# A new written-out order for 2455 events, and 214 zero products in place of 240, in a delta-rule attention with a feed-forward layer

## The chip, the core and the metric

The kernel runs on one core of a Trainium2 chip. The core has five engines with a queue of their own: PE (TensorE, matrix products), DVE (VectorE), ACT (ScalarE), POOL (GpSimd) and SP (SyncE, which here only issues DMAs). Each engine works its queue in order; an instruction that waits holds up all behind it. The metric is the device time of one execution in microseconds (us), the median of several; lower is better.

## The reference

```
k_n = k / (norm(k) + 1e-6)                      # 4 batches, 8 heads, 768 steps, 48 wide
for t in range(768):                            # state is 48 x 48 for each batch and head
    y[t]  = q[t] @ state
    v_old = k_n[t] @ state
    state = state + beta[t] * outer(k_n[t], v[t] - v_old)
x = y as 3072 tokens x 384
h = x @ w_in                                    # 384 x 2048
out = (h * erf(softplus(h))) @ w_out            # 2048 x 384
```

## The kernel before

**Attention.** The 768 steps are cut into 12 chunks of 64. For a chunk c the kernel loads k (`load_step`), its transpose (`load_kf`) and q (`load_q`), forms products of keys with keys and with queries on PE (`gram_mm`, names pg and pq), scales them on DVE (`gram_a`, `gram_p`), sends the result through DRAM to another layout (`to_dram`, `to_blocks`, tile gb) and solves a triangular system of 31 rows, two chunks at a time (`solve_row`): chunks 0 and 1 on DVE, all others on POOL. `back_t`, `merge_*` put the inverse together; `chain_u`, `chain_s`, `chain_y` carry the state from chunk to chunk, one event for each chunk and batch.

**Weights.** w_in and w_out come as 12 pieces of 512 KB each (`w_load`). ACT rescales each (`w_mask`, `w_sign`), DVE joins the bits (`w_bits`), and `w_mx` (ACT, one piece on DVE) takes the largest value. From the maximum of all twelve, `w_max`, `w_all` (a product on PE) and `w_scale` make one scale, which `w_idsc`, `w_hi`, `w_lo1` and the rest need to split the weights into two 16-bit parts. The first solve, `solve_row` of group 0, stands on DVE behind `w_scale` of w_in.

**Feed-forward.** Four chain events make one group of 256 tokens, 12 groups. `x_max` to `x_lo` scale and split the group. `ffn1` (9 products) gives 128 of the 2048 columns; two such make a unit of 512 values in one of two PSUM buffers (ph). For each unit ACT does Softplus (`e_sp`), then Erf (`e_erf`); the two need different function tables, and a table load stands wherever the function changes (line 165). DVE multiplies (`e_mul`, which frees ph), `e_split` and `e_rest` make the 16-bit parts H, and `ffn2` (6 products) adds to the output.

**Zero products.** `warm`, `fill` (line 180) and `fill2` (line 186) multiply zeros by zeros, 128x128 by 128x512. No result uses them. 15 stand at the start; the other 240 are events that stand in the order wherever PE is thought to wait.

**The order.** Every piece of work is an event. The list of events is built with due times, but these are not used for the order: the tuple ORDER names the events one by one, and each puts its instructions at the end of its engine's queue. ENG names the 17 events that do not run on their usual engine.

```
for i in range(WU):
    on(us(6 + 0.17 * i), fill)
for i in range(WV):
    on(us(6 + 0.17 * (WU + i)), fill2)
...
ev = [ev[i] for i in ORDER] if ORDER else sorted(ev, key=lambda e: e[:2])
for _, i, fn in ev:
    cur[0] = i
    fn()
```

A DMA on SP also waits until the DMA eight places ahead of it in the queue has landed, and until its buffer is free: for w_in there are six buffers of one kind (H) and five of another (L).

Of the kernel before, what the change touches and what calls it, by code (L numbers as in the profile page):

```python
# [46 lines left out]
DZ = 64
WG = -6
WU = 177
WV = 63  # L50
MT = 58
M1 = 0
WL = (0.9, 0.95, 1.0, 1.05, 1.1, 1.15, 24, 24.1, 31.0, 32.5, 34.0, 35.5)
WK = (6.0, 6.7, 7.4, 8.1, 8.8, 9.5, 28, 29, 36.0, 37.5, 39.0, 40.5)
WF = (6.6, 7.3, 8.0, 8.7, 9.4, 10.1, 28.6, 29.6, 36.6, 38.1, 39.6, 41.1)
WI = (17.0, 18.0, 19.0, 20.0, 21.0, 22.0, 31, 32, 50.5, 52.1, 53.7, 55.3)
WOT = (36, 38, 40, 42, 76, 78, 62, 86, 88, 90, 72, 74)
WD = 0.4
# [28 lines left out]
def delta_ffn_kernel(ctx, tc, kT, qT, ktok, vtok, btok, w_in, w_out, cst, out):  # L87
# [20 lines left out]
    def on(t, fn, *a, **kw):  # L108
        ev.append((t, len(ev), lambda: fn(*a, **kw)))
# [24 lines left out]
    def us(x):  # L134
        return (x - T0) / SW
# [671 lines left out]
    on(-98, warm, WARM)  # L807
# [4 lines that stand above are left out]
    on(us(0), clear_q)  # L812
# [229 lines left out]
```

## Time and profile before

| what | value |
|---|---|
| median of 3 runs | 613.57 us (609.68 to 617.38) |
| the profiled execution | 615.59 us, of which the span of instructions is 613.8 us |
| PE busy in the span | 595.4 us (97%), 49.5 us of it `warm` and `fill`, 15.8 us `fill2` |
| ACT busy | 522.9 us (85%), 216.8 us of it 169 table loads of line 165 |
| DVE busy | 403.8 us (66%) |
| POOL busy | 307.8 us (50%) |

The first product of the feed-forward that goes on without a wait starts at 97.35 us. Lines are those of the kernel file: 697 is `ffn1`, 749 to 751 `ffn2`, 719 `e_sp`, 724 `e_erf`, 728 `e_mul`, 685 `x_lo`, 355 and 357 `solve_row`, 301 `gram_a`, 287 and 291 `gram_mm`, 558 `w_load`. A busy PE may be busy with zeros, so its share says little; what counts is when useful products can run.

### The profile page before, as it was taken

What the parts mean: (1) busy time and instruction counts of PE and PEld (TensorE: products, weight loads), DVE (VectorE), ACT (ScalarE), POOL (GpSimd) and SP (SyncE); (2) the same over time, 40 slices, a digit from 0 to 9 for tenths busy, and PEclk for the clock granted to TensorE, in tenths of its full rate; (3) what the DMA queues carried; (4) which work ended last, traced back from release to release, by engine and by line L of the source; (5) the groups of instructions that cost most, each with busy time, mean ns of one, the idle gap of its engine ahead of it and who ended that gap; (6) DMA issues with size and microseconds to landing.
All of it is one profiled execution on the core that took longest, in us unless ns stands there. A gap on an engine that the chain in (4) does not pass through costs nothing.

```text
span 613.8 us, 25249 instructions
## 1 busy us (share of the span) xinstructions
PE 595.4 (97%) x11019; PEld 426.9 (70%) x11019; DVE 403.8 (66%) x926; ACT 522.9 (85%) x751; POOL 307.8 (50%) x484
## 2 busy tenths in 40 slices
PE   9899989999999899999999999999999999999996
PEld 3654456667777677777777777777777777777773
DVE  0769986668787788887776977666565655436221
ACT  8859897999996789878968999897989797989873
POOL 3000313798589733998527884489953122213221
PEclk9799898999999899999999999999999999999999
DMA  9999625850755367624485226713045200100111
GB/s 313 281 235 350 152 52 124 226 141 28 185 105 142 93 163 153 156 63 117 92 212 140 67 66 148 148 50 91 1 115 121 53 17 21 27 2 14 27 27 26
DMA packets 86382, 69.72 MB, mean 114 GB/s; under 512 B 64064, under 2 KB 73408, under 8 KB 86272
## 3 DMA queue, kind: packets, MB, share of 16 engines
q1 hardware_dynamic: 86272, 68.12, 43.1%
q8 instruction: 86, 1.41, 1.0%
q14 instruction: 24, 0.20, 0.1%
HBM read 48.17 MB, written 18.87 MB: 109 GB/s over the span
## 4 chain that ended last, share of the span: by engine, by line
PE 72%; POOL 7%; DVE 5%; DMA 5%; ACT 5%; issue 4%; SPq 1%; POOLq 0%; DVEq 0%; ACTq 0%
PE ph L697 25%; PE pr L749 9%; PE pr L751 9%; PE pr L750 9%; PE warm L180 3%; POOL xb L357 3%; POOL tmptmpg L355 2%; PE pc L485 2%; DMA qp<-qT 2%; PE pc L511 2%; PE pm L448 2%; DMA k<-ktok 2%; PE pc L515 2%; PE pc L499 2%; PE pg L291 1%
## 5 line engine op out<-in xcount | busy, mean ns | idle before, releaser
L165 ACT ACT_TABLE_LOAD x169 | 216.8, 1283 | 3.0
L697 PE MATMUL ph<-xh,w_in 128*128 128x256 f16 x1152 | 206.8, 274 | 0.1
L697 PEld LDWEIGHTS <-w_in 128*128 128x128 f16 x1728 | 166.5, 98 | 30.5 <-issue 2.2
L697 PE MATMUL ph<-xl,w_in 128*128 128x256 f16 x576 | 157.8, 274 | 1.2 <-DVE xl L685 1.2
L118 POOL TENSOR_TENSOR H<-L,H 128x512 f16<-128x512 f32 x58 | 69.3, 1203 | 134.6 <-DVE H L125 89.8
L749 PE MATMUL pr<-w_out,H 128*128 128x384 f16 x384 | 126.1, 328 | 0.0
L750 PE MATMUL pr<-w_out,H 128*128 128x384 f16 x384 | 125.7, 327 | 0.0
L751 PE MATMUL pr<-w_out,H 128*128 128x384 f16 x384 | 125.7, 327 | 0.0
L728 DVE SCALAR_TENSOR_TENSOR L<-ph,L 128x512 f32<-128x512 f32 x96 | 65.8, 687 | 88.9 <-ACT L L724 74.7
L118 POOL TENSOR_TENSOR z<-v,nm 64x192 f32<-64x192 f32 x94 | 51.8, 551 | 99.9 <-DMA v<-vtok 86.0
L357 POOL TENSOR_TENSOR xb<-xb,tmptmpg 128x31 f32<-128x31 f32 (+15 forms) x154 | 90.7, 589 | 12.1
L355 POOL TENSOR_TENSOR tmptmpg<-gb,xb 128x31 f32<-128x31 f32 (+15 forms) x154 | 83.6, 543 | 24.4 <-DMA gb<-d 11.2
L719 ACT ACTIVATE L<-ph,xct 128x512 f32<-128x512 f32 x96 | 65.4, 687 | 29.3 <-PE ph L697 25.9
L724 ACT ACTIVATE L<-L 128x512 f32<-128x512 f32 x96 | 59.9, 629 | 0.9
L751 PEld LDWEIGHTS <-H 128*128 128x128 f16 x384 | 37.6, 98 | 25.1 <-issue 0.2
L749 PEld LDWEIGHTS <-H 128*128 128x128 f16 x384 | 37.5, 98 | 22.8 <-issue 0.2
L750 PEld LDWEIGHTS <-H 128*128 128x128 f16 x384 | 37.6, 98 | 20.2 <-issue 0.2
L180 PE MATMUL warm<-zero 128*128 128x512 f16 x192 | 49.5, 412 | 1.2 <-DVE zero L171 1.2
L491 DVE TENSOR_TENSOR z<-pc,ga 64x192 f32<-64x192 f32 x88 | 31.2, 355 | 18.1 <-PE pc L485 16.4
L123 ACT CAST H<-L 128x512 f16<-128x512 f32 x56 | 33.5, 610 | 8.0 <-DVE L L728 7.9
L504 DVE TENSOR_TENSOR z<-pc,z 48x192 f32<-48x192 f32 x80 | 28.3, 353 | 17.3 <-PE pc L499 14.0
L180 PEld LDWEIGHTS <-zero 128*128 128x128 f16 x192 | 18.9, 104 | 25.6 <-issue 7.2
(159 smaller groups left out, 857.1 us busy)
## 6 DMA issues: line engine op xcount, KB each, us to landing
raw_in<-w_in SPq DMA_DIRECT2D x12, 512.0 KB, 7.1
raw_out<-w_out SPq DMA_DIRECT2D x12, 512.0 KB, 6.5
d<-A SPq DMA_DIRECT2D x22, 256.0 KB, 3.4
d<-pp SPq DMA_DIRECT2D x10, 512.0 KB, 3.7
qp<-d SPq DMA_DIRECT2D x20, 256.0 KB, 4.9
k<-ktok SPq DMA_DIRECT2D x12, 384.0 KB, 4.9
kpg<-kT SPq DMA_DIRECT2D x24, 192.0 KB, 4.5
qp<-qT SPq DMA_DIRECT2D x24, 192.0 KB, 3.6
```

The source lines that it names most:

```text
L118: {"V": ve, "G": ge}[pick(d)].tensor_tensor(*a, **kw)
L165: se.add_instruction(mybir.InstLoadActFuncSet(name=nc.get_next_instruction_name(), act_func_set_id=i, ins=[], outs=[]))
L180: te.matmul(wp[0], zero[:, :P], zero, start=True, stop=True)
L355: eng.tensor_tensor(tv, G[:, s, s + 1:].unsqueeze(1).broadcast_to([P, ncol, nr]), Xv[:, :, s:s + 1].broadcast_to([P, ncol, nr]), op=ALU.mult)
L357: eng.tensor_tensor(Xv[:, :, s + 1:], Xv[:, :, s + 1:], tv, op=ALU.add)
L697: te.matmul(ph, w[:, i, kt * P:kt * P + P], G[x][:, :, ksl], start=(m == 0), stop=(m == 8))
L719: se.activation(unit(g, u), G["ph", u], AF.Softplus, bias=0.0, scale=G["ct"])
L724: se.activation(Lu, Lu, AF.Erf, bias=0.0, scale=1.0)
L728: ve.scalar_tensor_tensor(Lu, fg[g]["ph", u], HSC, Lu, op0=ALU.mult, op1=ALU.mult)
L749: te.matmul(G["po"][a], gh[:, o, asl], wout_h[:, i, :], start=(i == 0), stop=False)
L750: te.matmul(G["po"][a], gh[:, o, asl], wout_l[:, i, :], start=False, stop=False)
L751: te.matmul(G["po"][a], gl[:, o, asl], wout_h[:, i, :], start=False, stop=(i == NFF - 1))
```

## The change

ORDER is a new permutation; the numbers of WU and WV fall from 177 and 63 to 167 and 47, so 26 zero products are gone. All other events are the same, and as 26 events fewer stand ahead of most, their numbers in ORDER and ENG fall by up to 26. The 17 events of ENG are the same and on the same engines.

```diff
-ORDER = (1321,1,1276,1266,2,3,4,5,
...
+ORDER = (222,1265,1280,1260,1,1250,224,1267,1251,1252,2,3,4,5,
...
-ENG = {350: "G", 464: "V", 734: "A", 742: "A",
...
+ENG = {324: "G", 438: "V", 708: "A", 716: "A",
...
-WU = 177
-WV = 63
+WU = 167
+WV = 47
```

On PE, 83 zero products stand ahead of the first useful product where 73 stood. Behind the first `ffn1` pair there stood 5 of line 180 and 63 of line 186; now there stand 1 and 47. The first place to look at is PE near the start, the products of `gram_mm` for chunks 0 and 1 (pg and pr2 are key by key; pr0 key by query, which needs qp, the loaded q). Before, where 16 rows alternate between the two halves of qp:

```order
L287 MATMUL pg1_0_284<-kpg1_200 64x64 x16
L287 MATMUL pg0_0_304<-kpg0_301 64x64 x16
L287 MATMUL pr0_81<-qp0_0_86,kpg0_301 64x64
L287 MATMUL pr0_81<-qp0_1_87,kpg0_301 64x64
...
L287 MATMUL pg0_1_345<-kpg0_301 64x64 x16
L287 MATMUL pr2_83<-kpg1_200 64x64 x16
```

Now, with 12 zero products between the fourth row and the fifth:

```order
L287 MATMUL pr2_83<-kpg1_117 64x64 x16
L287 MATMUL pg1_0_310<-kpg1_117 64x64 x16
L287 MATMUL pg0_0_336<-kpg0_329 64x64 x16
L287 MATMUL pg0_1_355<-kpg0_329 64x64 x16
...
L287 MATMUL pr0_81<-qp0_0_86,kpg0_329 64x64
L287 MATMUL pr0_81<-qp0_1_87,kpg0_329 64x64
...
L548 MATMUL spin_494<-ident_84,m1_in_106 128x128
```

The two products with q that stood among the key products now stand behind them all. Between the key products and the next ones with q there stood 22 zero products; now there stand 12, and then 16 ahead of the product of `w_all` (spin), where 10 stood.

On SP, the start of the queue (kpg is the transposed k, k the keys, raw_in a piece of w_in, qp the loaded q, d the way out through DRAM). Before:

```order
L558 DMA raw_in1_270<-w_in 128x1024
L275 DMA kpg0_301<-kT 48x1024 x2
L218 DMA qp0_0_86<-qT 48x1024
L218 DMA qp0_1_87<-qT 48x1024
L558 DMA raw_in3_384<-w_in 128x1024
L199 DMA mask_85<-cst 128x64
L200 DMA ident_84<-cst 128x128
L558 DMA raw_in10_391<-w_in 128x1024
L558 DMA raw_in5_393<-w_in 128x1024
L218 DMA qp1_0_88<-qT 48x1024
L218 DMA qp1_1_89<-qT 48x1024
```

Now:

```order
L275 DMA kpg0_329<-kT 48x1024 x2
L558 DMA raw_in1_333<-w_in 128x1024
L558 DMA raw_in7_375<-w_in 128x1024
L558 DMA raw_in10_383<-w_in 128x1024
L558 DMA raw_in9_387<-w_in 128x1024
L218 DMA qp0_0_86<-qT 48x1024
L218 DMA qp0_1_87<-qT 48x1024
L218 DMA qp1_0_88<-qT 48x1024
L218 DMA qp1_1_89<-qT 48x1024
```

All twelve pieces of w_in now stand ahead of q, and mask and ident moved to the seventh and eighth place of the queue.

On ACT, units 5 and 6 of the first group (L719 is Softplus, L724 Erf). Before:

```order
L165 ACT_TABLE_LOAD
L719 ACTIVATE L0_2_2072<-ph0_5_2025,xct0_1349 128x512
...
L724 ACTIVATE L0_2_2072<-L0_2_2072 128x512
...
L719 ACTIVATE L0_3_2190<-ph0_6_2168,xct0_1349 128x512
...
L724 ACTIVATE L0_3_2190<-L0_3_2190 128x512
```

Now:

```order
L165 ACT_TABLE_LOAD
L719 ACTIVATE L0_2_2045<-ph0_5_1985,xct0_1407 128x512
...
L719 ACTIVATE L0_3_2151<-ph0_6_2084,xct0_1407 128x512
L165 ACT_TABLE_LOAD
L724 ACTIVATE L0_2_2045<-L0_2_2045 128x512
...
L724 ACTIVATE L0_3_2151<-L0_3_2151 128x512
```

The two Softplus now stand ahead of the two Erf, with two table loads where there were four. The same is done for units 2 and 3 and units 6 and 7 of group 1, and units 0 and 3 of group 10: 8 loads fewer, 162 in all with the first one, where there were 170.

## Rows read from the trace of the kernel before

**Rows 1.** Busy time by stretch: us, then PE, PEld, DVE, ACT, POOL, clock, DMA share, GB/s.
```profile
20.00:24.00 4.00, 2.45 (x49) 2.02 (x47) 3.32 (x7) 3.73 (x8) 0.00 (x0) 0.81 1.02 247
24.00:28.00 4.00, 4.00 (x80) 4.00 (x79) 2.88 (x8) 3.21 (x9) 0.00 (x0) 0.50 0.95 322
28.00:32.00 4.00, 4.00 (x28) 1.96 (x25) 2.99 (x6) 3.51 (x8) 0.00 (x0) 0.50 0.71 173
...
38.40:66.40 28.00, 27.94 (x247) 14.47 (x245) 24.72 (x77) 22.02 (x43) 1.11 (x2) 1.00 0.98 313
66.40:97.30 30.90, 26.05 (x860) 16.78 (x859) 28.05 (x78) 25.82 (x64) 8.46 (x14) 0.94 0.32 78
97.30:165.00 67.70, 66.71 (x1164) 47.06 (x1164) 46.49 (x98) 63.47 (x84) 49.04 (x82) 0.97 0.54 138
165.00:272.00 107.00, 103.51 (x2566) 77.54 (x2563) 89.14 (x204) 89.83 (x132) 74.11 (x125) 0.98 0.55 133
272.00:613.70 341.70, 335.50 (x5866) 250.86 (x5866) 197.38 (x432) 289.71 (x371) 169.27 (x251) 1.00 0.30 71
```

**Rows 2.** The same stretch, zero products of line 186 alone: PE, PEld, clock, DMA.
```profile
97.30:165.00 67.70, 15.81 (x63) 5.58 (x63) 0.97 0.54 138
```

**Rows 3.** The same stretch, zero products of line 180 alone.
```profile
97.30:165.00 67.70, 1.25 (x5) 0.41 (x5) 0.97 0.54 138
```

**Rows 4.** The same stretch, table loads of line 165 alone, on ACT.
```profile
97.30:165.00 67.70, 30.79 (x24) 0.97 0.54 138
```

**Rows 5.** The chain of waits in order of time: start us, us, what.
```profile
14.74 8.85 DMA qp<-qT
23.73 1.83 PE pr L287 x29
...
29.08 6.67 PE warm L180 x22
...
37.76 2.27 PE warm L180 x10
...
97.35 3.59 PE ph L697 x17
...
103.94 2.07 PE ph L697 x18
...
107.60 1.08 PE pr L186 x5
```

**Rows 6.** SP in order of time: start us, us, line, out<-in.
```profile
17.98 0.33 SPq L200 DMA_DIRECT2D ident<-cst  x1
22.19 0.80 SPq L558 DMA_DIRECT2D raw_in<-w_in  x2
```

**Rows 7.** DMA issues of the page: count, KB each, us to landing.
```profile
raw_in<-w_in SPq DMA_DIRECT2D x12, 512.0 KB, 7.1
...
qp<-qT SPq DMA_DIRECT2D x24, 192.0 KB, 3.6
```

**Rows 8.** ACT in order of time; idle time before, and what ended it, in brackets.
```profile
30.00 0.67 ACT L565 ACTIVATE w_in<-raw_in 128x512 f32<-128x512 f32 x1 [0.49 <-DMA raw_in<-w_in]
...
35.96 0.66 ACT L587 ACTIVATE raw_in<-w_in 128x512 f32<-128x512 f32 x1
...
101.69 1.28 ACT L165 ACT_TABLE_LOAD   x1
102.98 0.63 ACT L724 ACTIVATE L<-L 128x512 f32<-128x512 f32 x1
```

**Rows 9.** DVE in order of time.
```profile
38.42 0.14 DVE L596 TENSOR_REDUCE m_in<-mx_in 128x1 f32<-128x1 f32 x1
...
40.29 0.29 DVE L612 TENSOR_REDUCE m_in<-spin 128x1 f32<-128x128 f32 x1 [1.08 <-PE spin L548]
...
42.18 0.18 DVE L355 TENSOR_TENSOR tmpT<-gb,xb 128x31 f32<-128x31 f32 x1
```

**Rows 10.** PE's own waits from 97.3 us on: us in total, times, longest.
```profile
PE pc L515 <- issue: 2.8, 2, 2.3
```

More of the change, by code (lines that the diff above doesn't have):

```diff
@@ L35 @@
-ENG = {350: "G", 464: "V", 734: "A", 742: "A", 759: "V", 766: "A", 796: "A", 913: "V", 1027: "V", 1134: "V", 1295: "V", 1437: "V", 1441: "G", 1445: "G", 1639: "A", 1981: "V", 2151: "V"}
+ORDER = (222,1265,1280,1260,1,1250,224,1267,1251,1252,2,3,4,5,6,7,8,9,10,11,12,13,14,15,16,17,18,19,20,21,22,23,24,25,26,27,28,29,30,31,32,33,34,35,36,37,38,39,40,41,42,43,44,45,46,47,48,49,50,51,1269,52,53,54,55,56,57,58,59,223,60,61,62,63,64,65,66,67,68,69,70,1253,1254,1281,1261,1262,1263,1282,1283,1295,1297,1270,218,228,1264,229,219,230,231,1284,220,232,1255,1257,233,234,1271,235,1266,1256,1258,1272,1273,1240,1241,236,237,258,259,256,257,1296,221,227,1245,1246,251,252,253,254,1247,1248,1275,217,1298,1276,1290,1291,1277,1285,1286,1287,1288,225,226,255,71,72,73,74,75,260,279,1242,1243,76,77,78,79,80,81,1268,82,284,285,286,277,1274,83,84,85,86,87,88,89,90,1292,278,1293,1244,1289,91,92,93,94,95,96,97,98,1299,1249,1278,1279,287,1294,1259,1360,1355,1361,1362,1364,289,291,290,292,1363,1365,1315,1367,1368,1320,1366,294,295,1370,1371,1373,296,297,298,1369,299,300,301,302,1372,1374,1376,1377,1379,1380,1375,1382,1383,1378,1385,1386,1388,303,304,305,306,307,308,99,100,101,102,103,309,310,311,312,313,314,315,316,1350,1381,1384,881,882,855,856,1321,1389,1391,1392,1387,1394,1395,1390,1397,1398,1393,104,105,106,107,108,1325,1326,1396,1400,1401,1399,1316,1403,1404,109,238,1330,1331,1332,1333,1340,1341,1300,1302,317,318,319,320,321,1322,1351,1317,838,1327,1328,1406,110,111,112,113,114,115,116,117,118,119,120,121,122,123,1345,288,240,325,241,124,125,126,127,839,1352,1402,239,1405,282,128,657,129,130,1357,131,132,1335,1336,1337,322,323,1338,1346,324,133,134,1353,1356,135,136,137,138,139,293,242,1347,1407,326,331,329,1318,334,332,1409,330,327,140,141,1348,328,658,243,1329,1310,1311,335,333,244,336,1349,342,847,1312,245,337,1313,283,659,660,661,343,246,341,142,143,1358,144,864,1410,381,407,662,145,146,1408,281,663,1305,664,1411,665,848,849,865,280,338,247,840,1334,339,147,1319,148,149,1323,889,850,1342,150,151,841,340,1301,872,152,666,852,844,845,1343,153,154,866,1339,1303,867,1354,1344,155,156,853,157,158,1359,1324,248,857,858,249,869,870,846,871,261,263,854,873,159,160,1306,161,162,906,344,1307,861,862,1308,163,164,250,262,863,165,264,265,268,667,1314,1447,1448,1309,266,166,167,1304,1412,1413,668,669,168,1449,1451,347,1453,1414,1452,1454,1415,842,345,1416,890,269,270,1417,1418,267,1455,1457,1487,1488,272,273,276,169,670,843,859,672,860,1459,671,1461,1492,1493,1419,1420,170,171,898,899,271,274,673,172,1489,346,907,851,868,675,1463,1465,674,348,349,350,1494,351,352,353,354,676,1497,1498,173,174,175,176,177,178,179,180,181,182,183,874,184,185,875,883,878,884,1490,677,879,880,355,356,357,358,1499,1467,1469,900,901,1502,886,1503,1421,397,876,1471,398,1473,359,360,361,362,887,877,681,1504,382,915,1422,891,1423,1475,903,892,893,895,1507,186,187,188,189,190,191,192,1424,1425,1426,1491,1508,1509,1427,193,194,195,196,1477,1512,894,904,197,275,1479,198,199,200,201,202,203,204,1481,916,1456,1495,1496,1458,1460,1428,905,885,902,888,1429,896,897,1531,1500,1501,1517,1513,1430,1431,1514,1505,394,1518,1519,1532,1533,1432,385,1510,205,206,207,208,209,395,1520,383,1535,210,1536,923,924,384,386,1433,1434,388,1483,1537,1538,1511,1485,1522,1462,1464,389,1435,1523,1436,1524,1547,1549,1581,211,680,1551,212,213,214,396,215,408,1525,1437,409,391,410,411,1553,1586,1582,1583,363,364,365,366,1584,453,1587,932,1506,1466,1468,1470,1472,412,1438,1539,1541,1439,1474,1515,467,367,413,392,1571,1572,368,369,476,678,370,371,372,216,949,373,374,375,376,377,378,379,387,380,1588,1543,390,1440,1441,399,1516,400,1585,950,1573,1545,1576,1577,1574,1476,402,403,1555,1557,1442,416,1443,393,1478,679,406,940,1450,1521,1480,1526,1591,414,415,933,695,1578,1559,682,683,1444,1589,1590,1579,1580,1445,941,1575,417,418,419,420,421,422,423,424,425,426,427,1446,401,685,684,1592,1593,1482,1484,1486,1527,1529,428,429,430,431,432,433,434,1561,694,1596,686,687,697,688,404,1597,957,1540,1542,689,691,698,1598,699,701,700,1594,1599,1600,1544,1546,1548,690,1563,908,1595,692,693,702,703,917,1567,1569,1534,909,1565,1601,1606,918,910,920,704,919,912,913,921,911,934,710,935,925,1528,1530,1550,1552,937,435,926,929,1602,1603,1607,1608,1604,927,922,914,436,437,930,928,966,938,939,958,936,1554,705,707,931,1605,1615,1616,706,696,1617,1556,942,967,943,951,466,1558,1560,1562,1619,1621,952,712,1622,1620,405,438,439,440,441,708,709,946,463,442,1609,464,450,451,452,465,944,945,991,1631,454,1633,1665,443,444,954,955,947,445,446,447,1666,974,975,959,1564,477,478,968,1647,1649,713,960,963,479,969,961,971,1685,729,1686,1667,953,448,711,970,972,1651,1653,1690,962,964,480,1687,455,457,481,1566,482,456,458,460,1635,461,1637,1610,459,462,1668,714,468,1691,1692,1688,1693,1670,1671,992,1672,1673,1674,1669,469,715,717,716,1623,1625,1655,948,965,1008,1009,1639,1694,1641,1675,470,449,718,720,983,471,1568,1656,483,956,973,1699,472,473,719,1570,1611,1700,1676,1657,1658,1701,721,723,725,1677,1659,1643,1000,475,722,724,1703,1704,1705,1706,1645,1627,1629,1680,1660,1681,1678,984,485,1017,519,520,1001,1661,976,977,484,985,1624,1626,986,1682,1683,1684,980,978,979,486,487,488,489,1662,1663,988,987,981,1664,1707,1709,1002,1003,993,1739,1715,1717,474,994,727,1005,1740,1025,1741,1679,1026,989,730,982,990,521,997,745,1006,1613,995,998,996,1731,1004,1733,1628,1630,999,1632,1634,1749,1007,1783,1769,532,1770,1771,1784,1750,1751,726,1785,1723,533,534,731,1742,1725,1759,1727,490,1752,491,1729,1764,733,522,523,732,734,1765,545,546,547,744,1612,735,524,742,526,1760,1761,1636,1638,1787,1789,1640,1642,548,549,550,492,493,1018,494,1790,736,737,739,738,740,741,1644,535,1711,1713,1744,1745,1646,1034,1772,551,525,527,1766,1010,1011,1719,1721,495,496,497,728,498,499,500,501,1754,1746,591,1755,1735,502,528,1035,529,1689,530,1019,1020,503,504,505,1014,1788,1756,1036,1737,1037,1015,506,507,508,1774,1775,509,1648,1650,1762,1767,1768,510,1012,1013,511,1776,1039,1040,1041,1022,1021,1618,1027,1028,1799,1801,1833,1803,1805,1652,512,513,1614,514,1763,1023,1838,1029,1038,1834,1835,1702,1654,536,1042,1031,537,1839,1840,1791,1793,1757,531,515,516,1695,1032,1747,1748,517,1059,1743,1795,1797,1836,1837,1773,1823,1824,539,1825,1033,1030,1043,538,1708,1710,1828,1712,1714,1829,1830,1826,743,746,1807,1809,1843,1844,1811,1813,1753,540,542,541,747,1758,1848,1024,1716,1718,1845,1846,748,518,749,1815,1817,1853,1831,1051,1786,761,1841,1842,1827,750,752,1720,1722,1016,1867,1777,1778,751,1868,1052,588,552,1869,544,753,1849,1850,1060,1871,755,1872,1724,1726,1728,1730,1873,553,1854,604,554,555,556,557,1085,1086,754,1053,756,757,1044,1874,1855,1856,1857,589,1832,1045,1870,759,1061,1062,1891,758,1893,1895,1897,1732,1065,543,558,1054,1851,1847,1068,1069,1927,614,1932,1046,1734,1055,1928,1929,1048,1930,1056,1049,1057,1697,1047,1819,1821,1070,1933,1934,1102,1103,1899,1901,1736,1858,1859,1937,1852,1738,1071,559,560,561,562,1073,1063,605,1698,762,763,1860,1779,1792,1875,1877,1794,1796,1074,1075,1066,1067,1931,1938,1050,1939,1935,601,1058,1951,1064,1883,1907,1908,764,592,1072,602,1780,1798,1800,590,765,1885,1909,1952,603,615,1953,766,606,608,1917,1903,760,1918,768,1802,767,563,564,565,566,1905,1942,616,1804,1919,1920,769,771,1955,567,568,569,570,571,572,1887,1889,1806,1076,1861,773,617,1808,1862,1921,772,1943,1810,770,1944,1940,1812,1814,1879,618,619,1881,609,1922,573,574,1923,620,607,1957,1077,1078,1912,1924,575,576,577,1956,1958,1816,1967,611,1969,610,1925,1079,1082,1913,2001,1087,1104,1093,1094,1914,1781,2002,1971,1973,578,612,2003,774,1818,1959,1088,1083,1080,1105,1107,1081,2006,2007,579,580,1089,1961,581,2008,582,1820,1696,1782,1926,1095,1096,1945,1991,1090,1091,1963,583,1099,1910,1136,584,1153,1911,1097,613,1822,1098,1992,1100,1108,1993,1109,1092,1084,1101,2035,585,586,1137,1965,1863,593,594,595,1154,1876,1996,1983,596,1985,587,1915,1916,1946,1878,1880,777,1997,1106,1119,775,2021,2022,1120,597,778,779,1998,2023,600,2036,2037,1975,1977,781,780,1882,1936,1994,2011,1884,1110,1999,2024,782,784,783,2025,1886,1888,2012,785,788,2013,1890,791,1892,1979,1981,2004,2039,2041,2040,2042,789,2000,2014,786,2038,787,2016,1894,1896,1138,1111,623,1112,621,1995,1941,622,624,625,626,627,628,598,2015,1121,2017,2018,2019,1122,790,1127,1864,2009,1898,1900,629,2043,1113,2045,2020,1114,776,1116,1124,2075,2076,2059,1170,1115,1123,2061,1902,1904,2095,794,1139,1141,1117,1125,2077,1126,1118,2096,2097,1987,1989,2026,2027,2028,2098,1128,1129,795,797,630,631,632,633,634,635,1171,1144,2047,2049,2080,1906,2063,2065,1947,793,1130,1133,1865,796,798,1960,1962,1964,2005,1187,2099,2100,0,2101,2102,1142,1134,1135,2081,2051,2103,2053,1143,800,1131,2082,2085,2086,799,636,2119,2120,2121,2087,2055,2057,637,638,639,1954,2104,640,641,1145,1966,1968,2090,2067,2069,2091,1140,2092,2010,1132,801,803,802,1970,642,643,2123,1972,2125,1974,2124,792,644,645,646,647,1976,1978,2105,2106,599,2126,2151,805,806,648,649,2107,2153,2071,650,651,2189,2190,2078,2083,804,2073,2110,2029,1172,1146,1948,2088,1155,2191,1980,1982,2155,1949,2157,2194,1950,1984,2030,1156,1147,1148,2079,1149,1986,2195,2196,2111,1157,652,2093,653,654,1988,2108,1990,1173,1161,1162,2135,2137,809,2031,2084,1150,2112,2169,1158,1151,655,1175,1163,1866,2139,2141,2044,2170,1159,1160,2171,2046,2174,2089,1188,2094,1178,2175,1195,2127,1164,1165,1176,1167,2129,2172,1196,2113,2176,2131,1168,2159,807,810,811,813,812,2033,2114,1179,808,1204,2034,1152,1177,824,1169,2133,2160,2161,2048,2164,2165,2050,2052,2054,2056,1174,2203,814,2204,816,2143,2145,2166,2147,2162,2205,2167,2149,2192,2207,2208,2209,2210,656,2179,2184,2058,2060,2062,2180,815,817,2181,818,2064,822,2227,2229,2185,2163,1205,2066,2109,2068,819,2168,2186,1189,2173,821,2182,1166,1219,1180,1181,820,1190,2263,2264,823,2231,2233,2268,2269,1220,1206,1184,1182,825,2070,2265,1191,1183,1233,2072,2074,1185,2115,2183,2219,2221,1207,2253,1197,1192,2270,2128,826,1193,1226,2254,1198,1186,2177,2255,2223,2225,2258,2259,1209,1201,1202,1203,827,2178,2193,1227,2235,828,2237,2130,2132,2134,2187,2188,2273,2136,2260,2116,2117,2118,2274,2275,2197,2266,2267,2211,2213,1210,829,2215,1211,2198,2217,2243,2248,1194,2287,2244,2288,2289,2138,2245,2291,830,1199,2292,2293,2249,2140,2271,2142,2144,2146,2294,2250,832,1208,2311,2313,2272,831,2256,2261,2262,833,2319,1234,834,2148,2347,2348,2276,2349,2246,2247,2251,2321,2357,2358,2303,2305,2150,837,835,2252,2337,2152,836,2154,2156,2158,2359,1200,2122,2199,1212,1213,2200,2307,1235,1214,1221,1215,2206,2290,2338,2309,2339,2340,2341,1222,2342,2212,2295,2257,2297,2327,2343,2344,2214,2216,2218,2220,2328,2329,2222,1236,2239,2241,2299,2301,2330,2332,2224,2278,2279,1216,1217,2333,2226,2228,2280,2230,1228,1223,1237,1224,1229,1230,1238,1225,1218,1231,1239,2334,1232,2371,2335,2323,2201,2325,2362,2281,2277,2282,2315,2363,2372,2373,2336,2375,2364,2377,2232,2317,2234,2345,2236,2238,2378,2240,2032,2376,2352,2242,2353,2379,2381,2354,2283,2331,2387,2389,2296,2298,2350,2411,2300,2412,2346,2413,2383,2421,2385,2302,2304,2306,2351,2422,2360,2361,2416,2284,2417,2365,2308,2423,2395,2355,2356,2418,2310,2391,2285,2393,2424,2426,2414,2427,2428,2429,2366,2286,2425,2419,2202,2420,2397,2431,2432,2312,2433,2314,2316,2318,2320,2322,2415,2324,2326,2367,2430,2403,2434,2368,2399,2401,2380,2382,2384,2405,2386,2436,2437,2435,2438,2369,2439,2440,2374,2370,2407,2409,2441,2442,2443,2446,2447,2448,2388,2390,2392,2394,2396,2398,2400,2402,2444,2445,2449,2450,2404,2406,2408,2410,2451,2452,2453,2454)
@@ L36 @@
+ENG = {324: "G", 438: "V", 708: "A", 716: "A", 733: "V", 740: "A", 770: "A", 887: "V", 1001: "V", 1108: "V", 1269: "V", 1411: "V", 1415: "G", 1419: "G", 1613: "A", 1955: "V", 2125: "V"}
 LEAD = 3
```

1 line of the change is left out of this document (removed).

## The prediction

> **What bounds the kernel now.** I read the windows by stage first. From 165 us on the reader sees PE busy for 103.5 of 107 us and then for 335.5 of 341.7 us, at a clock of 0.98 to 1.00, while ACT, DVE and POOL have room [rows 1]. So the last 449 us are PE's own work, and the order inside them is worth little. What is saved ahead of them comes off the end: all later work on PE moves up, and the others follow.
>
> Between 97.3 and 165 us PE looks as busy, 66.7 of 67.7 us [rows 1], but 63 of its products are those of line 186 and 5 those of line 180, and these are zeros: 15.81 us by the sum of their durations [rows 2, 3]. The durations overlap in the pipeline; the chain of waits has five in 1.08 us, so one takes 0.216 us of PE's time [rows 5], and 68 take 14.7 us. The engine that sets the pace in this stretch is ACT, busy for 63.47 of 67.70 us [rows 1], of which 30.79 us are 24 table loads of 1.283 us [rows 4].
>
> Ahead of 97.3 us the chain of waits starts with q's transfer (14.74, 8.85 us), then 29 products with q, and 22 zero products from 29.08 us that take 6.67 us, 0.303 us each [rows 5]. They are slow since PE waited in 20 to 24 us (busy 2.45 of 4.00) and its granted clock fell to 0.50, the lower of two levels, through 24 to 32 us [rows 1]. Meanwhile ACT works through the pieces of w_in; the last one lands at 30.00, and the last `w_mx` ends at 36.62 [rows 8]. The maximum follows only at 38.42, since DVE stands behind products that PE gives after the 22 zeros; 10 more zeros (2.27 us) stand ahead of `w_all`, whose result DVE reads at 40.29; the first solve starts at 42.18 [rows 5, 9]. From there DVE is busy for 24.72 of 28.0 and 28.05 of 30.9 us [rows 1]: it is this row of DVE work that sets when the first group's feed-forward can start, at 97.35 us [rows 5].
>
> **The change part by part.** *The pairs on ACT, first two groups.* Two of the three early pairs, units 5 and 6 of group 0 and units 2 and 3 of group 1, fall into 97.3 to 165 us: 4 loads x 1.283 = 5.1 us of the 63.47 go [rows 1, 4]. The third, units 6 and 7 of group 1, comes later, beside PE's own work, and I count it as nothing: PE hides it, and if that cover is gone it is a gain of 2.6 us more on ACT. The pair in group 10 lies near the end, beside a PE that is full [rows 1]: nothing. A pair also makes the first unit's Erf wait for the second's Softplus, 0.63 us and more later [rows 8], and so its multiply, its PSUM buffer and its `ffn2`.
>
> [...]
>
> *The zeros in the same stretch.* 68 become 48: 20 x 0.216 = 4.3 us of PE [rows 2, 3, 5]. They were there because PE would have waited for ACT; ACT now asks for 5.1 us less, so the cover reaches, by 0.8 us. I take 4.3. The lower end is 0: the products wait in place of the zeros. Above it lies the first unit: 17 products of `ffn1` took 3.59 us at the start, 18 took 2.07 a little later [rows 5]. Should PE reach it warm, it saves some 1.6 us more: upper end 5.9.
>
> *The start.* Ten zeros more stand ahead of PE's first useful product, 10 x 0.216 = 2.2 us; its start was 19.1 us, so the key products come at some 21.3 instead. They wait for kT anyway then, and now run in one piece, with the products of q behind them and 12 zeros between. If PE isn't idle, its clock stays at 1.00 there. I take no cost for the ten, as PE waited in that place for 1.55 of 4 us [rows 1]; if the cover is gone they cost 0.6.
>
> On SP two transfers of q, 192 KB each, no longer stand ahead of the last w_in pieces, and SP issued the last two of these at 22.19, after 3.9 us in which nothing was issued [rows 6, 7]. 384 KB at the 322 GB/s of that stretch [rows 1] are 1.2 us; the upper end is the whole hole, 3.9. Queued behind the twelve are q (four transfers) and, later, the way through DRAM (gb); they land later by what w_in gains, and the q products after them. ACT, though, now does two more `w_mx` behind the last mask, 2 x 0.66 = 1.3 us [rows 8]. So the last `w_mx` ends between 0.1 us later and 2.6 earlier than 36.62.
>
> From the last `w_mx` to the solve it takes 42.18 - 36.62 = 5.56 us now. 1.80 of it is DVE late for the maximum, behind the 22 zeros [rows 8, 9], 12 of which stay and would be done in 2.6 us at full clock instead of 6.67 [rows 5]. I put DVE in time; then 16 zeros instead of 10 stand ahead of `w_all`, but they start earlier and are done when the maximum is. The tail is then some 3.9 us, a gain of 1.6; what is late next is the product of `w_all` itself and `w_scale`. The start of the solve so gains 1.6 to 4.2 us; the first feed-forward follows by as much only if DVE's row holds. The operations in it are the same, and it has 3.3 + 2.9 us free in 59 [rows 1], which may take up 1 us more or less; against it, transfers share 0.98 of their engines in 38.4 to 66.4 [rows 1], where w_out arrives, and this stream may hold the gain back by up to 1.6 us. Ends: 0 and 5.2. I take 3.2, nearer to the row of SP's hole than to none.
>
> *The rest.* Of the zeros, +10 ahead of the first product, -10 between the key products and q, +6 ahead of `w_all` and -20 from the first `ffn1` pair on leave 12 of the 26; these 12 stood between 42 and 97 us, where PE has 0.06 + 4.85 us of idle and DVE sets the pace [rows 1]: nothing. A wait of PE of 2.3 us at the products of line 515, for which the trace shows no data missing [rows 10], I leave as it is.
>
> **Sum.** 3.2 + 4.3 = 7.5 us. Against the profiled execution (615.59; span 613.8) this gives 608.1. That one lies 2.0 above the median of the three, 613.57, inside their spread; the saving is the same on any, so on the median: 613.57 - 7.5 = **606.1**. The sum's own ends, 0 and 5.2 + 5.9, would give 613.6 and 602.5; both terms at an end together are unlikely, and I put the forecast's own range at 603.5 to 608.5.
>
> **The rivals.**
>
> *A, the front gives nothing.* The transfers set the solve either way: share 0.98 for, the idle 3.9 us of SP against [rows 1, 6]. Only the zeros go: 613.6 - 4.3 = 609.3.
>
> *B, the zeros become waits.* PE waits for ACT or DVE in 97.3 to 165 as long as the zeros took. For it: ACT at 63.47 of 67.70, and the Erf of a pair's first unit comes later. Against it: 5.1 us less of loads. Only the front counts: 613.6 - 3.2 = 610.4.
>
> *Both, or the order does nothing it seems to:* 613.6.
>
> *C, slower: the clock.* Without zeros PE is idle while it waits for a pair, and the clock falls as it did behind the wait at 20 to 24 us, to 0.50 for about 10 us [rows 1]. Each such stretch costs about 5 us of PE's work; three of them in 97.3 to 200 turn the saving into a loss, four give 613.6 - 7.5 + 20 = 626.1. The deciding point is 15 us more at the lower level. Against it: 48 zeros still stand there, and the clock was 0.97 [rows 1]. [...]
>
> *D, more is gained.* Both terms at the upper end, and the 2.3 + 0.5 us of line 515 go as well [rows 10]: 613.6 - 5.2 - 5.9 - 2.8 = 599.7.
>
> **How the numbers follow.** Forecast 606.1: 0.50. A, 609.3: 0.13. B, 610.4: 0.13. Both, 613.6: 0.07. C, from 613.6 up: 0.07. D, 599.7: 0.10. The range leaves out C and most of D, and reaches over A, B and the case of nothing: 601.5 to 613.6. Two per cent, about what a measurement of this kernel can tell from no change, are 601.3 and 625.8. Faster by more: D and a tail of the forecast, 0.11. Slower by more: the half of C with four stretches, 0.03. The rest, 0.86, is within.
>
> **What the profile of the changed kernel would show.** The last piece of w_in lands ahead of 30.0 us and the first solve on DVE starts at 38 to 40.5, not 42.18. The key products run in one piece at 21 to 26 us, at a clock of 1.00 in the place of 0.50. The first `ffn1` starts near 94. In the stretch behind it there are 20 table loads instead of 24 and 47 products of line 186, some 10.2 us; PE has no new wait for ACT or DVE there. From 165 on PE is as full as before. A is right if the solve starts at 42 still; B if PE's waits in the feed-forward's first 68 us add up to 3 us or more beyond those of before; C if stretches of 0.50 appear behind 97 us. I would be wrong beyond the range if the new order brings a wait into the last 449 us, which I took as moved whole, or frees more there than PE's idle 9.7 us allow.

## The result, and the profile after

The changed kernel takes 617.94 us (median of 20 runs, 613.74 to 622.02); the kernel before, on the same chips, 613.75 us (20 runs, 608.01 to 622.18). The ratio is 1.0074, 95% interval 1.0048 to 1.0100: 4.5 us slower, where 606.1 was forecast. Ratios here and below leave out executions more than 1.5% above the fastest of their kernel, so they can differ from the quotient of the medians, which are of all runs.

The profiled execution of the changed kernel took 613.74 us (span 611.7), which is the fastest of its 20, so the two profiles alone, 613.74 after 615.59, point the wrong way. Its windows, with the columns and most of the stretches of [rows 1]:

```profile
20.00:24.00 4.00, 4.00 (x83) 2.87 (x83) 3.61 (x15) 4.00 (x8) 0.00 (x0) 1.00 1.00 393
24.00:28.00 4.00, 4.00 (x72) 2.71 (x68) 3.90 (x11) 2.05 (x4) 0.00 (x0) 1.00 0.92 250
38.40:66.40 28.00, 26.40 (x224) 12.86 (x222) 25.96 (x68) 25.30 (x50) 4.47 (x8) 1.00 1.04 315
66.40:97.30 30.90, 26.15 (x912) 17.83 (x915) 27.58 (x76) 23.30 (x59) 8.18 (x12) 0.89 0.39 96
97.30:165.00 67.70, 62.90 (x1105) 45.17 (x1097) 48.21 (x99) 60.26 (x83) 49.99 (x81) 0.97 0.51 125
165.00:272.00 107.00, 100.69 (x2640) 76.41 (x2639) 86.03 (x202) 84.45 (x125) 77.21 (x132) 1.00 0.60 142
```

Most of what the prediction wanted to see is there. At 20 to 28 us PE is busy at a clock of 1.00, where it waited and fell to 0.50 before. In the order of time, ACT, then DVE, then the chain of waits (answers to [rows 8], [rows 9] and the `ffn1` row of [rows 5]):

```profile
28.08 0.67 ACT L565 ACTIVATE w_in<-raw_in 128x512 f32<-128x512 f32 x1 [0.71 <-DMA raw_in<-w_in]
...
34.83 0.66 ACT L587 ACTIVATE raw_in<-w_in 128x512 f32<-128x512 f32 x1
```
```profile
35.60 0.16 DVE L602 TENSOR_REDUCE m_in<-mx_in 128x1 f32<-128x11 f32 x1 [1.53 <-ACT raw_in L587]
...
39.23 0.18 DVE L355 TENSOR_TENSOR tmpT<-gb,xb 128x31 f32<-128x31 f32 x1
```
```profile
94.47 2.02 PE ph L697 x17
```

The last piece of w_in is there at 28.08 instead of 30.00; the tail from the last `w_mx` (35.49) to the solve is 3.7 us, where 3.9 was estimated; the solve starts at 39.23 and the feed-forward at 94.47. Behind 97.3 us the zeros of line 186 and the table loads have shrunk, answering to [rows 2] and [rows 4]; the 13.12 us are a sum of durations like the 15.81 before, and the 21st load falls into this window because the feed-forward starts 2.9 us earlier:

```profile
97.30:165.00 67.70, 13.12 (x47) 4.72 (x47) 0.97 0.51 125
```
```profile
97.30:165.00 67.70, 25.85 (x21) 0.97 0.51 125
```

Two signs are wrong, and they are the case. PE is less full than before, 62.90 of 67.70 and 100.69 of 107 us against 66.71 and 103.51 [rows 1]. And the list of its waits from 97.3 us on, which began with [rows 10] in the kernel before, now begins (us in total, times, longest):

```profile
PE pc L515 <- issue: 3.6, 3, 2.3
PE pz L431 <- issue: 1.5, 1, 1.5
PE sp L548 <- DVE xm L658: 1.2, 1, 1.2
PE pe L416 <- DVE T L405: 1.1, 2, 0.6
PE pq L291 <- DVE pp L308: 0.8, 2, 0.6
PE pc L485 <- issue: 0.8, 1, 0.8
PE pr L750 <- issue: 0.7, 1, 0.7
```

6.6 us of these are "issue", a wait for nothing that the profile names. Where they lie tells what they are. PE in order of time, in the kernel before and then in the changed one, the same products of the state chain:

```profile
112.26 0.89 PE L485 MATMUL pc<-z,xm 128*32 128x48 f32 x64
113.08 0.82 PE L186 MATMUL pr<-zero 128*128 128x512 f16 x3
113.83 0.43 PE L511 MATMUL pc<-qp,z 128*32 128x64 f32 x16
114.08 0.41 PE L515 MATMUL pc<-qp,z 128*32 128x64 f32 x16
114.42 0.82 PE L186 MATMUL pr<-zero 128*128 128x512 f16 x3
...
116.12 0.28 PE L515 MATMUL pc<-qp,z 128*32 128x64 f32 x5
116.99 0.41 PE L515 MATMUL pc<-qp,z 128*32 128x64 f32 x11 [0.59 <-issue]
```
```profile
114.41 0.43 PE L515 MATMUL pc<-qp,z 128*32 128x64 f32 x16 [1.06 <-issue]
...
119.16 0.28 PE L515 MATMUL pc<-qp,z 128*32 128x64 f32 x5
121.74 0.41 PE L515 MATMUL pc<-qp,z 128*32 128x64 f32 x11 [2.30 <-issue]
122.09 0.57 PE L499 MATMUL pc<-z,k 64*48 64x48 f32 x32
```

PE stops in the middle of 16 equal products, behind the fifth, which speaks against a wait for data. Counted in PE's queue from its first weight load, with weight loads, products and semaphore instructions all as one each, the stop stands ahead of instruction 4033 = 193 + 256 x 15, and the other "issue" stops of over half a us stand ahead of 3777, 5825, 6081 and 9921, which are 193 + 256 x k as well (to within two places, as the trace leaves the order of neighbours open). The trace also has a DMA queue of instructions, in the page's part 3:

```profile
q8 instruction: 86, 1.41, 1.0%
```

PE's queue has 22,113 instructions in this trace (10,993 weight loads, as many products, 127 semaphore instructions). The numbers 193 + 256 x k fall into it 86 times, once for each of the 86 transfers of 16 KB; the kernels with more instructions further below have 87 of both (one stands at the very edge, 87 and 86). Worked out from the transfers and PE's instruction numbers (us; gap is the time from the start of PE's last instruction of a block to that of the next one):

```
kernel   ends at   transfer starts   transfer ends   end reached   gap    PE goes on
before     3777        114.23           115.48         116.18      0.80     116.99
before     7105        200.78           201.72         200.50      2.47     202.97
after      3777        111.97           113.15         113.13      1.28     114.41
after      4033        118.92           120.23         119.22      2.52     121.74
after      5825        174.91           176.24         176.52      1.02     177.54
after      6081        179.83           180.75         181.25      0.97     182.23
after      9921        257.22           258.61         258.22      1.72     259.94
```

In these rows PE goes on 2.2 to 2.8 us after the start of the block's transfer, 1.2 to 1.5 us after its end. The traces of all 20 profiles bear this out: behind the first `ffn1` they have 83 gaps over 0.5 us at such places, and 80 of them end 1.2 to 1.9 us after the end of the block's transfer, whether the gap is 0.5 or 3.9 us long; of the other three, two end later, with a wait for DVE. By these rows PE stands where it runs through what is left of the block ahead in less than the 2.2 to 2.8 us. 64 products of line 485 are 128 instructions in 0.89 us, so the state chain can; `ffn1`, with two instructions in 0.11 us, takes 7 us for 128. Between the chain's products shown above there stood three zeros and three again, which now stand elsewhere or are gone, and other block ends now cost time: in the kernel before, 4033 falls on a zero of line 186, and neither there nor at 5825 does PE stand. The five gaps of the changed kernel in the table add up to 7.5 us.

### The profile page after: what moved, and what is told of

The parts are those of the page before. It is cut to its first block, busy times and chain, and to the rows that moved or that the text cites. A ratio compares the mean times of both kernels' runs of the same rounds, so it can differ in the third digit from the quotient of the medians.

```text
span 611.7 us, 25194 instructions
## 1 busy us (share of the span) xinstructions
PE 585.7 (96%) x10993; PEld 421.4 (69%) x10993; DVE 404.7 (66%) x926; ACT 512.7 (84%) x743; POOL 309.7 (51%) x484
## 4 chain that ended last, share of the span: by engine, by line
PE 75%; ACT 8%; DMA 5%; DVE 5%; issue 3%; POOL 3%; SPq 0%; POOLq 0%; ACTq 0%; DVEq 0%
PE ph L697 28%; PE pr L749 10%; PE pr L750 9%; PE pr L751 9%; PE pc L485 3%; PE pc L511 2%; PE pg L291 2%; PE pm L448 2%; PE pc L515 1%; PE pc L499 1%; DMA raw_in<-w_in 1%; PE pr L641 1%; PE pe L416 1%; PE pz L431 1%; POOL xb L357 1%
## 5 line engine op out<-in xcount | busy, mean ns | idle before, releaser
L719 ACT ACTIVATE L<-ph,xct 128x512 f32<-128x512 f32 x96 | 65.5, 687 | 35.4 <-PE ph L697 28.2
L118 POOL TENSOR_TENSOR z<-v,nm 64x192 f32<-64x192 f32 x94 | 53.1, 565 | 73.7 <-ACT w_in L130 39.4
L724 ACT ACTIVATE L<-L 128x512 f32<-128x512 f32 x96 | 59.7, 629 | 0.9
L180 PE MATMUL warm<-zero 128*128 128x512 f16 x182 | 45.6, 401 | 1.2 <-DVE zero L171 1.2
L180 PEld LDWEIGHTS <-zero 128*128 128x128 f16 x182 | 17.5, 102 | 23.0 <-issue 5.0
```

Of the source, the lines that this page charges most:

```text
L118: {"V": ve, "G": ge}[pick(d)].tensor_tensor(*a, **kw)
L180: te.matmul(wp[0], zero[:, :P], zero, start=True, stop=True)
L719: se.activation(unit(g, u), G["ph", u], AF.Softplus, bias=0.0, scale=G["ct"])
L724: se.activation(Lu, Lu, AF.Erf, bias=0.0, scale=1.0)
```

## The experiments

Three theories stood against each other. **P** is the prediction's sum. **I**: PE stands at ends of blocks, and the loss is where these ends fall. **C**: the clock, by rival C: with fewer zeros PE falls to the lower level more often.

**The two kernels again.** No edit.

> The kernel before, unchanged, for the granted clock of several executions and a second profile. Theory I (PE runs out of instructions): the profile again shows PE idle without a data wait exactly at its instruction number 193 + 256 x k (near 200 us and 116 us), 0.7 to 2.5 us each, with a 16 KB transfer of instructions that started less than 2 us ahead; the sum of such gaps is 4 to 6 us. Theory C (the clock alone): the spread from run to run, 608 to 622 us, follows the mean granted clock, and this kernel's median clock is higher than the 0.985 of the changed kernel. Time in both: 613.7, plus or minus 2.

> The changed kernel, unchanged, for a second profile, since its first one (613.74 us, clock 0.991) lay 4 us below the median of its 20 runs. Theory I: the profile shows gaps at instruction 193 + 256 x k that add up to more than 8 us (8.2 in the first profile, 4.8 in the kernel before), and stretches at clock 0.50 begin behind the longest of them. Theory C without I: more stretches at 0.50, but behind waits for data. Time in both: 618, plus or minus 2.

Measured: 613.30 us (12 runs), ratio 0.9995 (0.9958 to 1.0032); and 617.29 us (12 runs), ratio 1.0057 (1.0024 to 1.0090). The second profile of the kernel before has a different start. Its windows, as [rows 1]:

```profile
20.00:24.00 4.00, 2.63 (x73) 2.35 (x73) 3.43 (x9) 4.00 (x10) 0.00 (x0) 1.00 1.00 267
24.00:28.00 4.00, 4.00 (x75) 2.75 (x71) 3.56 (x6) 3.24 (x8) 0.00 (x0) 1.00 0.93 313
28.00:32.00 4.00, 4.00 (x59) 2.40 (x58) 3.65 (x7) 4.00 (x10) 0.00 (x0) 1.00 0.85 261
```

PE waits at 20 to 24 us as before (busy 2.63 of 4.00), but the clock stayed at 1.00, and DVE starts the solve at 37.91 instead of 42.18. So a wait there, which the prediction names as the cause, is not always followed by the lower level. The start on which the prediction's first term was worked out isn't this kernel's start in every execution. The median of the mean granted clock is 0.992 in these 12 runs of the kernel before and 0.985 in the 20 of the changed one. The clock is at 1.00 or at 0.50 all through the first profiles of the two kernels (before: 1.00 up to 22.5 us, 0.50 up to 32.7, 1.00 again up to 70.3). If it is so in all runs, that is (1 - 0.992) x 2 x 611 = 9.8 us at the lower level against 18.5, and half of the difference, 4.3 us, is as much as the whole loss. In the changed kernel's 20 runs the span grows by 0.6 us for each us at the lower level (correlation 0.82), but in the 35 runs of the kernel before that were timed beside these two only by 0.26 (0.56). So the clock can be worth anything from half of the loss to all of it, and C doesn't tell what brings the lower clock about.

**Moving nothing but the places of PE's instructions.** The first 16, 32, 48 or 64 zero products at the start are cut in halves, which adds twice as many instructions, 32 to 128 (the counter that picks them is left out here):

```diff
-            te.matmul(wp[0], zero[:, :P], zero, ...)
+            te.matmul(wp[0][:, :256], zero[:, :P], zero[:, :256], ...)
+            te.matmul(wp[0][:, 256:], zero[:, :P], zero[:, 256:], ...)
```

> The changed kernel, with the first 32 zero products cut into two halves of 256 columns: the same work, order and time on PE, but every later instruction of PE stands 64 places further back in its queue, so that the blocks of 256 end at other places of the program. Theory I: the gaps move to other products, and their sum changes by several us; the time moves by 2 to 6 us, in either direction. Theories that rest on the zero products' time, the clock or the data waits of the order: 618, plus or minus 1.5, as for the changed kernel itself.

> As the shift by 64, with 64 zero products cut in halves, so that all that follows stands 128 places further back in PE's queue. Theory I: another sum of gaps, a time that differs by 2 to 6 us from 618 or from the shift by 64. The other theories: 618, plus or minus 1.5.

> The kernel before, with the first 32 zero products cut into two halves each: same order, work and time on PE, all later instructions of PE 64 places further back. Theory I, in the form that the order before happens to stand well against the ends of its blocks of 256 instructions: 615 to 619, with gaps that add up to more than 7 us (4.8 and 5.6 in the two profiles of the kernel before). Theory that the places of the blocks don't matter: 613.5, plus or minus 1.5.

> As the shift by 64 of the kernel before, by 128 places. Theory I: 615 to 619 and more than 7 us of gaps; otherwise 613.5, plus or minus 1.5.

> The kernel before, with 16 zero products cut in halves: all later instructions of PE 32 places further back. Theory that the places make the loss: 614.5 to 618, as for 64 and 128. Theory that the order does: 613.5, plus or minus 1.5.

> As before, by 96 places. Theory that the places make the loss: 614.5 to 618; theory of the order: 613.5, plus or minus 1.5.

> The changed kernel, shifted by 32 places. Theory of the places: anything from 612.5 to 618, and the mean over the places 0, 32, 64, 96 and 128 within 1 us of that of the order before. Theory of the order: 617.5, plus or minus 1.5, and a mean 3 us or more above.

> The changed kernel, shifted by 96 places; the theories as for 32.

The halves take as long as the whole: in the order before, PE's first useful product starts at 18.9 to 20.0 us in all five places. Measured, as ratio to the kernel before (interval), median us, the median of the kernel before timed beside it (in brackets; the batches ran on different chips, so only these two compare), and the gaps at block ends behind the first `ffn1` in the one profile of each (at shift 0 the mean of two):

```
shift   order before                                   order after
  0     0.9995 (0.9958-1.0032) 613.30 (613.47) 4.6     1.0057 (1.0024-1.0090) 617.29 (613.47) 7.9
 32     1.0039 (1.0011-1.0068) 613.60 (611.63) 5.1     1.0094 (1.0065-1.0123) 617.69 (611.63) 8.2
 64     1.0051 (1.0013-1.0088) 617.98 (614.15) 5.2     1.0029 (0.9992-1.0065) 615.21 (613.47) 6.4
 96     1.0031 (1.0006-1.0056) 613.15 (611.63) 3.1     1.0052 (1.0015-1.0090) 615.44 (611.63) 6.8
128     1.0035 (1.0001-1.0069) 616.20 (614.15) 7.7     1.0059 (1.0028-1.0091) 617.41 (613.47) 5.8
```

All four shifts make the kernel before slower, by 0.31 to 0.51%, with every interval above 1, one of them barely (1.0001), and by the medians of all runs by 1.5 to 3.8 us, though no work or order is changed: the order before stands better at its own places than at any other that was tried. In before_shift64 a block ends in the products of line 485 (490 in its file):

```profile
199.29 0.87 PE L490 MATMUL pc<-z,xm 128*32 128x48 f32 x61 [0.18 <-DVE xm L460]
202.21 0.28 PE L490 MATMUL pc<-z,xm 128*32 128x48 f32 x3 [2.05 <-issue]
```

The mean of the five places is 1.0030 for the order before and, with the 20 and the 12 runs at place 0 put together as 1.0068, 1.0060 for the order after. So of the 0.68% at place 0 about half is the good place of the order before, and about 0.30% the order's own, with an uncertainty of some 0.2%. Before the last four runs two theories were set against each other, means within 1 us and means 3 us or more apart; 0.30% are 1.8 us, and with this uncertainty they decide for neither. Nor does the sum of gaps in one profile tell the ratio of its kernel: after_shift128 has fewer than before_shift128 and the higher ratio.

**The new order up to a cut, the old one behind it, and the reverse.** ORDER is put together from the two; zeros stand where each part has them.

```diff
-WU = 177
-WV = 63
+WU = 179    # new_to_solve; new_to_ffn: 171, 63; old_to_ffn: 173, 47
+WV = 63
```

> The new order as far as the first row of the first solve on DVE, and behind it the events that are left in the order before (242 zero products: 96 ahead of the cut, 146 behind). By the prediction the start alone gains 3.2 us: 610.3. By the profiles taken since, an undisturbed start of the kernel before reaches the solve at 37.9 us and the new order at 39.2: 614.8, plus or minus 1.5. A start that sets nothing: 613.5.

> The new order as far as the first product of the feed-forward, and behind it the order before (234 zero products: 166 ahead of the cut, 68 behind). By the prediction again 610.3. Theory C, in the place where I had put no cost (42 to 97 us, 6 zero products fewer behind the first two blocks of the triangular inverse): a stretch at the lower clock from 68 us on in the profile, the first product of the feed-forward near 94 to 96 us instead of 91.6, and 616.5 to 618. If the loss lies behind the cut (instructions that come late, waits where zeros stood): 613.5, plus or minus 1.

> The order before as far as the first product of the feed-forward, and behind it the new order (220 zero products: 172 ahead of the cut, 48 behind, and the pairs on ACT). By the prediction 20 zeros fewer give 4.3 us: 609.2. Theory that the zeros became waits of the same length: 613.5, plus or minus 1. Theory I (blocks of instructions that come late behind the cut cost more than before): 615 to 618, with gaps that add up to 4 us more than in the kernel before.

Measured: new_to_solve 1.0070 (1.0030 to 1.0109), new_to_ffn 1.0121 (1.0067 to 1.0176), old_to_ffn 1.0090 (1.0050 to 1.0131). P's 610.3 and 609.2 fall: none of the three is faster than the kernel before. How much slower they are is less sure than these intervals say. The medians of all runs are 615.04, 618.84 and 616.99 us against 614.58 for the kernel before timed beside them, 0.5, 4.3 and 2.4 us more, where the ratios give 4.3, 7.4 and 5.5. By the ratios the new front and the new rest cost 7.4 + 5.5 us and both together 4.2, and the parts don't add up; by the medians they cost 4.3 + 2.4, and no difference is shown. If there is one, each part's cost may depend on where the other leaves the block ends (the cut moves what stands behind it by 4 or 12 places), but that was not tested by moving them back. In the profiles of new_to_ffn and old_to_ffn the largest gap is at 3777 (3.32 and 2.93 us). Whether new_to_solve loses anything stays open.

**Zeros put back at 64 to 70 us in the changed kernel.** In the names of the events, as they stand in ORDER:

```diff
-    back_t 0,1 ... back_t 1,0 ... merge_e 0
+    fill x5, back_t 0,1 ... fill x4, back_t 1,0 ... fill x6, merge_e 0
```

> The changed kernel with 15 zero products put back in three places: 5 ahead of the second product group that turns the blocks of the first inverse, 4 ahead of the third, 6 ahead of the products of its merge, where PE sat idle at 64.5, 66.6 and 69.5 us. Theory C: the stretch at the lower clock from 68 to 75 or 78 us goes, the first feed-forward moves forward by 1.5 to 3 us, and the time falls by as much, to 614.5 to 616. Theory that DVE and POOL set the pace there anyway: 617.5, plus or minus 1.

Measured: 620.87 us, 1.0132 (1.0084 to 1.0181). The theory that zeros in this place hold the clock and bring the feed-forward forward falls. The lower level at 68 us went, but another stretch came at 78.6 to 82.0, and the first `ffn1` product ends at 95.9 us, not earlier. Behind it the gaps at block ends are 8.8 us, 3.4 of them at 5825: the 30 instructions more had moved the blocks again. All eleven profiles with the order before ahead of the first `ffn1`, but for one, have a stretch at the lower level between 63 and 76 us too; it isn't the change's.

**The second term by itself, on the order before.** The 20 zeros keep their place, but at 8 x 8 take little time (in before_pairs_thin20 the next product starts 0.05 us after the one at 112.78 us and 0.10 us after the one at 120.40, where a full one takes 0.216); for the pairs, three Erf stand behind the next Softplus.

```diff
-            te.matmul(pr[2], zero[:, :P], zero, ...)           # 16 of line 186; 4 of line 180 alike
+            te.matmul(pr[2][:8, :8], zero[:, :8], zero[:, :8], ...)
-    e_erf 0,5 ... e_sp 0,6          e_erf 1,2 ... e_sp 1,3          e_erf 1,6, e_mul 1,6 ... e_sp 1,7
+    ... e_sp 0,6, e_erf 0,5         ... e_sp 1,3, e_erf 1,2         ... e_sp 1,7, e_erf 1,6, e_mul 1,6
```

> The kernel before, in which the 20 zero products that the change takes out behind the first product of the feed-forward (4 of line 180, 16 of line 186, in proportion at their places) shrink from 128 x 512 to 8 x 8: the instructions of PE keep their places, but 20 x 0.2 us of its time is taken out. By the prediction's sum, without the pairs ACT isn't freed, and the products wait in place of the zeros: 613.5, plus or minus 1. If PE's time there counts whole: 609.5. Theory I and C (zeros leave time for instructions to arrive and hold the clock): 613.5 to 617, with longer gaps near 115 and 194 us or a new stretch at 0.50.

> The kernel before with the three early pairs on ACT alone; all 240 zero products keep their size. By the prediction the zeros hide the pairs: a ratio to the kernel before of 1.000, plus or minus 0.002. If ACT sets the pace in spite of the zeros: 0.9955, as with the shrunk zeros.

> The kernel before with the three early pairs on ACT of the change (units 5 and 6 of group 0, units 2 and 3 and units 6 and 7 of group 1, 6 table loads fewer) and with the same 20 zero products shrunk to 8 x 8; nothing else is moved. This is the second term of the prediction by itself: 613.5 - 4.3 = 609.2, plus or minus 1.2. Theory I and C: nothing of it arrives, 612.5 to 617, with the time of the zeros found again as PE idle at the ends of blocks and behind products that wait.

> The kernel with the three pairs and the 20 shrunk zeros, shifted by 64 places as the other shifts were (32 zero products at the start cut in halves). If the gain of 2.7 us and the loss of 3.1 us by this shift add up: a ratio of 1.0005, plus or minus 0.003. If the gain needs the places of the order before: 1.004 or more.

Measured: thin zeros alone 0.9994 (0.9958 to 1.0030); pairs alone 0.9995 (0.9962 to 1.0027); both 0.9955 (0.9924 to 0.9986), 611.41 us; both, shifted by 64 places, 1.0068 (1.0033 to 1.0103). Neither half alone shows a change, and together they give 2.7 us of the second term's 4.3. That each needs the other, as the term assumed, is not shown: the intervals of thin zeros alone and of both overlap, and their medians, timed side by side, are 612.32 and 611.41 us. The stretch of ffn units in before_thin20 and then in before_pairs_thin20, PE to DMA as in [rows 1]:

```profile
97.30:165.00 67.70, 66.06 (x1173) 46.35 (x1172) 48.38 (x100) 64.94 (x86) 49.06 (x81) 0.98 0.57 139
```
```profile
97.30:165.00 67.70, 63.25 (x1166) 45.02 (x1165) 46.12 (x99) 58.89 (x80) 48.05 (x81) 1.00 0.56 138
```

With thin zeros alone ACT is as full as before, 64.94 of 67.70; with the pairs it has room, 58.89. The version with both is faster than the two kernels. But 64 places further it is slower than the kernel before by 0.68%, 4.1 us, where the gain and the shift's own 0.51% would together give 1.0006; the difference of 0.62% is just outside its uncertainty of some 0.6%. So the gain holds at the places of the order before and is not found at the one other that was tried. Its profile has a gap in the same place as before_shift64, at 202.21 us; in both the block's transfer took 2.2 to 2.6 us, where the median over all profiles is 1.1:

```profile
202.21 0.28 PE L584 MATMUL pc<-z,xm 128*32 128x48 f32 x3 [2.16 <-issue]
```

## Why the prediction was wrong

**The start, 3.2 us: failed.** Its steps came true one by one (w_in, DVE in time, tail of 3.7 us), and the solve starts at 39.23 against 42.18. What failed is the sentence ahead of them, "the first solve starts at 42.18", taken as the kernel's own and not as that of one execution. Over the profiles of all runs, 11 with the order before ahead of the solve start it between 37.26 and 42.18 us, mean 39.7; 9 with the new order between 38.35 and 40.70, mean 39.5. The one on which the sum was made was the latest of the eleven. Where a start lies goes with the clock at 22 to 33 us: with no stretch at 0.50 there the order before starts the solve at 37.3 to 37.9 us (three profiles), with 10.2 us of it, as in the profile of the forecast, at 41.7 and 42.2 (two), and the other six lie between. The new order had no such stretch at 20 to 28 us in any profile, but undisturbed it starts the solve later than the order before does, at 38.35 to 40.25 us (seven). So the term was the price of one slow start, and the transfers gave nothing that shows. The end of the first `ffn1` product agrees in six profiles of each order (the two kernels and their shifts): 95.4 and 95.3 us in the mean, with a spread of some 2 us. Rival A, "the front gives nothing", came out right for another reason than the transfers, and not by its sign, a solve that starts at 42 still.

**The zeros and the pairs, 4.3 us: held by themselves, lost in this order.** By themselves they give 2.7 us (0.9 to 4.7, from the interval), so 4.3 is not excluded. From the first `ffn1` product to the 288th, six profiles of each order give 91.0 us before and 92.4 after. This is where rival B, zeros that become waits, came true: PE's idle time from 97.3 to 165 us grew from 0.99 to 4.80 us, 3.8 where B's sign was 3. But the waits are mostly not for ACT or DVE: the gaps at block ends behind the first `ffn1` are 5.0 us in the mean of six profiles before and 7.1 after, and the data waits of the list above come on top.

**"A wait of PE of 2.3 us at line 515, for which the trace shows no data missing, I leave as it is": failed.** This was the row on which the case turns [rows 10]. The 2.3 us are one of the gaps at block ends (7105), and its number in the queue, not its line, says where others will be. Leaving it constant while an order moves every instruction was the step without a reason. What it left out is measured: the same order costs 0.31 to 0.51% more at four other places.

**The 12 zeros that went between 42 and 97 us, costed at nothing:** nothing speaks against it; the same two means of 95.4 and 95.3 us would not show a difference of a us.

**Rival C: half right.** The clock is lower, 0.985 against 0.992, by about as much as the loss. In the changed kernel and its shifts a stretch at 0.50 starts at 119 to 124 us in all six profiles, each in or just behind a gap of 2.5 to 3.9 us at 3777, 4033 or 4289. In the six of the order before one starts between 110 and 130 us once, at 110.8, and none of them has a gap over 1 us there. That PE waits for its instructions in these gaps is read from the 1.2 to 1.9 us between the end of the block's transfer and the end of 80 of the 83 gaps. That the lower level follows from the gap is argued from the order of the two alone: a gap of 2.85 us at 194 us in before_again was followed by no such stretch, nor was one of 3.4 us at 176 us in after_zeros68. That the missing zeros have no part in it is not shown either. The prediction's price of this rival doesn't add up: by its own 5 us for a stretch of 10, two stretches turn the saving of 7.5 us into a loss, not three, as its 15 us at the lower level say.

**A reading.** The 15.81 us that the prediction gives for 68 zeros are the 63 of line 186 alone [rows 2]; the 5 of line 180 have 1.25 more [rows 3]. Its sum goes by 0.216 us a zero and isn't touched; its 10.2 us for 47 zeros is such a sum, and the row that it was to be seen in has durations, 13.12.

**What stays open:** which waits make up the 0.30% that is the order's own, about half of the loss, and whether the front alone costs anything.

## What to carry to other kernels

A wait that the profile calls "issue" in the middle of equal products is a place to count instructions: here such waits stood at 193 + 256 x k, and 32 to 128 instructions more at the start, with which PE's first useful product still started at 18.9 to 20.0 us, made the kernel before slower by 0.31 to 0.51%. Before costing a term on one profiled execution, look whether the stretch repeats in a second one; here two executions of one kernel, with the clock at 0.50 for 10.2 us of the start and not at all, lay 4 us apart at the solve. A gain under 1% in a kernel of very many small products should be timed at two or three shifted places before it is believed.

## What was not expected of the hardware

Behind the first `ffn1` PE stood at 83 ends of blocks of 256 instructions in the 20 profiles, for 0.5 to 3.9 us each, as in before_shift64 for 2.05 us behind 61 small products of line 485 that took 0.87 us. How late the next block's transfer starts goes with the data transfers: over two profiles of each kernel, it starts 0.7 us (median) after PE enters the block ahead when the 16 DMA engines were busy for under 0.05 of the 2 us before, and 1.7 us (at most 4.7) when for over 0.95. What in the transfers makes it later, no run here shows.
